# Attention with inducing points and a gated feed-forward network: the first quad over another queue, the last quad in quarters, the exponential sums as one more column, and a later schedule

## The chip, the cores and the metric

The kernel runs on one core of one Trainium2 chip. The metric is the device time of one execution in microseconds (us), and lower is better. Every number below comes from a timed execution or from the profile of one execution.

Engines are named as the profile names them: PE is the matmul engine (PEld its weight loads), DVE the vector engine, ACT the scalar engine, POOL and SP the two that also issue most of the DMAs. "x" of 2048 tokens (16 rows on each of 128 partitions) is called a quad.

## The reference

There are four batches of 12416 tokens with 128 features, 32 inducing points, and a feed-forward width of 1536.

```python
def mab(q, kv):                              # one attention, kv is key and value
    a = np.exp(scale * (q @ kv.T) - max)     # max along the row
    a /= a.sum(-1, keepdims=True) + 1e-09
    return a @ kv
h   = mab(I, x)                              # 32 inducing points look at all tokens
att = mab(x, h)                              # all tokens look at the 32 results
out = (sigmoid(att @ w_gate) * (att @ w_val)) @ w_out
```

So each batch has a first stage that must see all of x (`h`, 32 rows), and a second one that is cheap per token. The feed-forward network on 49664 tokens is nearly all of the work.

## The kernel before

Batch 0's first stage is a prologue, done as fast as the six quads of x arrive. Then come 97 output blocks of 512 tokens. A list of words, one word for each block, tells in which order PE gets its matmuls: `G` and `A`/`B` are gate and value products, small letters the output products, and `J` takes the next small job of a later batch (scores `s1`, sums `h`, scores of the second stage `s2`). The events `at(n, k, ...)` say in which block n and at which of its four steps k the other engines get their instructions.

The row of the first stage is `sum(exp * x) / sum(exp)`. The numerator is 16 matmuls of 32 output rows each, on four column tiles of PE (r = 0 to 3). The denominator is a set of four matmuls with a matrix of ones as weights, into the 128 columns beside it, so that DVE later adds 256 columns for each quad:

```python
def h_mm(ps, b, q, first, last, tail, ch=0, cs=P):
    for j in range(4):                                  # the sums
        nc.tensor.matmul(ps[:, cs:cs + P], ones[:, 0:P], a1n[(b, q)][:, j, :], ...)
    ...
    for j in range(4):
        for r in range(4):                              # exp * x
            nc.tensor.matmul(ps[r * M:(r + 1) * M, ch:ch + P],
                             a1_chunk(b, q, 4 * r + j), xqs[(b, q)][:, ts(4 * r + j, P)], ...)

def h_add(ps, b, first):                                # one add for each quad, on DVE
    nc.vector.tensor_tensor(out=haccs[b][:], in0=haccs[b][:], in1=ps[:, 0:2 * P], op=ALU.add)
```

The second stage's weights reach the feed-forward products by a long chain, called the rep chain below. There is one for each batch and each pair of quads, eleven in all after batch 0's first pair:

```python
def rep_events(n, b, d):
    put(n, 1, "s2", b, d)               # PE scores, ACT exp
    at(n + 1, 0, e2_dma, b, d)          # DMA transpose -> e2n
    at(n + 2, 0, s2_sum, b, d)          # POOL: row sums -> rs
    at(n + 3, 0, s2_rec, b, d)          # DVE:  1 / rs -> rc
    for i in range(2):
        at(n + 3, 0, a2_mul, b, d, i)   # POOL: e2n * rc -> a
        at(n + 3, 1, a2_dma, b, d, i)   # DMA transpose -> a2T
        at(n + 3, 3, rep_put, b, d, i)  # DMA to DRAM -> dt
        at(n + 4, 2, rep_get, b, d, i)  # 4 DMAs back -> rep
```

In one block out of four (5, 9, 13 and so on to 93) POOL also computes some of the gate-value products (`vt` and `x` below). Those blocks are called shared here.

The prologue's loads are issued by POOL, which casts fp32 to fp16 on the way (the cast queue): six quads, the sixth in two halves, then the three weight matrices of the network. SP issues two small fp32 loads, the inducing points and x's last 128 tokens (`xt`).

The softmax here doesn't subtract the row's maximum and nothing guards it: scores larger than these inputs give would overflow.

Of the kernel before, what the change touches and what calls it, by code (L numbers as in the profile page):

```python
# [16 lines left out]
P = 128  # L17
# [8 lines left out]
    "GAGBWGAabGBcGAfeGBdGAhBWgJG AilkjBGAJaBbGAcGBfeGAdWBhgG AilGBkGAjBGGAbaBcfGAeGdBG "  # L26
    "AhGBgiGAkljBGGAbaBcfGAGedBGh AGBgGiAGkBljGAGBabcGAeGBfdG AgGBhiGAlkjBWGAbafBJe "
    "AGBdcGhgAGilkjBJAGaWBbGAceBGfG AdhBGgAGikBljGAGaBbceAGfdGBhG AgiGBlGAkjJBGAGabBGcGAefBdJG "
    "AhBJgiAGlkBjJAGabBcfeG AGdhBgGAilkjBGGAabBcefGAdWBhgG AilkjBGGAbacBGAfGBedGAGhgBiG "
    "AlkGjBJAGBGbacGAefGBdGAJBJG AhgBGiAGklBjGAGBbafe AGdhBGgAGicBGlAGkBjJAGbWBaG "  # L30
    "AcGBfeGAdhGBgGAilWBkGAjJBGJabc AGBJfeAGdBGhgGAilkjBGGAbBJa AGceBGfAGdBhGgAGilkBjG "
    "AGBbafeAGdgGBhcGAikljBGGAabcBfG AeGBdgGAhiGBlGAkjBWGAabcBGef AGdhBGgAGilBGAGkjBWGAbacBefG "
    "AdGBhgGAilkjBGGAabBfeG AGBdcgGAhGiBlkjAGBWabcGAeBJf AGdgBGhAGilkBjAGGBabcfAGedBGgh "
    "AGikljBJGAbGBacGAfeGBdGAGhgBiG AlJBkGAjJBGAGbafBWe AGdhgBGAGiBclkjAGGBabcfAGedBGh "
    "AGgiBGkAGljBJAGBaWbcGAfeGBdg AGhiGBlGAkGBjGABWabAGcBJfG AedhBGAGgiBlkjAGGBabef "
    "AGdcBGgAGhiBkljGAGBbaceAGfdgBG AGhikBljGAGBabcGAefBWdAGhgGBi AGlkBjJGABbGacGAeGBfGAGdhBJ "
    "AGBJgiAGlkjBJAGabfBeG AdWBhgGAiGcBlkjAGGBabceAGfdBWg AGhikBGAGlBjGAGBbacfAGedBGhgG "
    "AiBGklGAjJBGAGabcfBGAGBGed AGhgBiGAGlkjBJGABWfeb AGadGBgGAhiGBcGAkljJBGAbaGcGBefG "
    "AdhGBgGAilkjBGGAabcBeGAfJBG AdGhBGAgJBiGAlGkBjGAGBabcf AGedBGgAGhilBkjGAGBbafe "
    "AGdcBGhAGgiBGkAGljBWAGBbacfG AedGgBhGAikGBljAGGBbacAGfBedG AGhgiBGAGBkljAGGBbacGAfGBedG "  # L40
    "AhgGBiGAkljBWGAabeBfG AdGBchGAgJBiGAlkjBWGAabBcfeG AGdgBhGAilkjBGGAabcBefGAdGBghG "
    "AilkjBJGAbGBacGAfGBeGAGdBhgG AiGBlkGAJjBJAGBWbaf AGedGBhGAgiGBcGAklBjWAGabBcfG "
    "AeGBdhGAgiGBlkAGjJBGAGabcBGe AGfBdGhAGgilBkjAGGBabcGAeGfBdG AhJBgGAilkjBGGAbaBfedG "
    "AcGhBgGAilkjBGGAabcBefGAdGgBhG AikljBGGAbacBGAfWBedGAhGgBiG AlkGBGAjJBGAGbaBcWGAfedBJ "
    "AGBJhgGAilkjBGAJaBbG AeWBfdGAcgGBhGAilkjBGGAabcBfeG AdgGBhGAilkjBGGAbacBGfAGedBGh "
    "AGgiBGkAGlBjJAGBGabcAGGBfG AeGdBgGAhGBikGAljBJG AefdGBaGAbhGBgGAicBGkJljAGBGbacG "
    "AfeBGdGAhgGBiGAklBjGAJbBaG AcGBfeGAdGBhgGAilkjBGGAaBJb AGcfBGeAGdhBGgAGilkBjG "
    "AGBbafeAGdhGBgGAciBkljGAGBabceG AfdGBhgGAilkjBGGAabcBeGAfGdBG AhGgBiGAlkjBGGAbaBcfGAGeBGd "
    "AGhBgGiAGlkjBGAGBefba AGdhBGgGAicBkljGAGBabcfAGedGBgG AhikBljGAGBbacGAefBWdAGhgBGi "
    "AGlkBjGAGBbacGAefGBdGAhGgBiG AlkjBGGAfeBabGAJdBhG AgGiBcGAlkjBGGAabcBfGAeWBdhG "  # L50
    "AgGBikGAljGBGAabcBefGAGBdhgG AilGkBjGAGBbacAGefdBGAGgGBhG AilBkjAGGeBfbaGAdhWBgG "
    "AicBGkGAlBJjGAGBabcGAfeBdgG AGhBikljGAGBabcGAfBWeGAdBhGgG AilkBjAGGaBbcGAefGBdGAGhBgiG "
    "AklBjGGAbaBfeGAJBdhG AgGiBcGAlkjBGGAbaBcfeGAdWhBgG AilkjBGGAabBcGAGfeBdGAhGBgiG "
    "AlkjBGGAbaBGcAGfedBGAGhGBgG AilkBjGAGefBbaGAdhBWgG AicBkljGAGBabcGAefGBdAGhgBGi "
    "AGlkjBGAGBbacGAfeBWdGAhgBGi AGlkBjGAGBbacGAefGBdGAhgGBiG AlkjBGGAfeaBbdGAgWBhiG "
    "AclkjBGGAabBcGAGfBedGAhGgBiG AlkjBGGAbaBcGAfWBedGAhGgBiG AlkjBGGAbaBcGAGBfedGAGhgiBG "
    "AkljBGGAabBfedGAgWBhcG AikljBGGAbacBGAGfeBdGAhGgBiG AlkjBGGAbaBcGAfWBedAGhgGBi "
    "AlkBGjABbAacBefdAghBilkj"
# [5 lines left out]
def kernel(  # L64
# [83 lines left out]
    xt32 = const.tile([P, C], F32, tag="xt32")  # L148
    nc.sync.dma_start(xt32[:], x[0, ds(NT0, P)])
# [6 lines left out]
    load_x(0, 0)  # L156
# [10 lines left out]
    for half in range(2):  # L167
        nc.gpsimd.dma_start(
            xl[:, ts(half, QT // 2)],
            x[0, ds((NQ - 1) * QT, QT)].rearrange("(p j) c -> p (j c)", j=QT // P)[  # L170
                :, ts(half, QT // 2)],
        )
    nc.gpsimd.dma_start(wg16[:], moe_w_gate.rearrange("c (j f) -> c j f", f=P))
# [10 lines left out]
    haccs = [pers.tile([P, 2 * P], F32, tag=f"hacc{b}", name=f"hacc_{b}") for b in range(B)]  # L184
# [63 lines left out]
    def h_mm(ps, b, q, first, last, tail, ch=0, cs=P):  # L248
        for j in range(4):
            nc.tensor.matmul(  # L250
                ps[:, cs:cs + P], ones[:, 0:P], a1n[(b, q)][:, j, :],
                start=first and j == 0, stop=last and j == 3,
            )
            if tail and j == 0:
                nc.tensor.matmul(
                    ps[:, cs:cs + M], ones[:, 0:P], a1n[(b, "t")][:], start=False, stop=False
                )
        for j in range(4):
            for r in range(4):
                nc.tensor.matmul(  # L260
                    ps[r * M:(r + 1) * M, ch:ch + P],
                    a1_chunk(b, q, 4 * r + j),
                    xqs[(b, q)][:, ts(4 * r + j, P)],
                    start=first and j == 0,
                    stop=last and j == 3 and not (tail and r == 0),
                )
        if tail:
            nc.tensor.matmul(
                ps[0:M, ch:ch + P], a1n[(b, "t")][:], xtail[:, b, :], start=False, stop=last,
            )  # L270

    def h_add(ps, b, first):
        if first:
            nc.vector.tensor_copy(out=haccs[b][:], in_=ps[:, 0:2 * P])
        else:
            nc.vector.tensor_tensor(
                out=haccs[b][:], in0=haccs[b][:], in1=ps[:, 0:2 * P], op=ALU.add
            )
# [3 lines left out]

    recs = {}

    def hfin_rec(b, sums):
        hs = smp.tile([P, M], F32, tag="hs", name=f"hs_{b}")
        nc.vector.reduce_sum(
            out=hs[:], in_=sums.rearrange("p (r m) -> p m r", m=M), axis=AX.X
        )
        rec = smp.tile([P, M], F32, tag="rec", name=f"rec_{b}")  # L290
        nc.vector.reciprocal(out=rec[:], in_=hs[:])
        recs[b] = rec

    def hfin_dve(ps, b):
        nc.vector.tensor_tensor(out=hTs[b][:], in0=recs[b][:], in1=ps[:, 0:M], op=ALU.mult)
# [284 lines left out]
    def xT_pe(b, q, half):  # L580
        ps = slot_g(f"xt_{b}_{q}_{half}")
        v = ps[:].bitcast(F16)
        for j in range(8):
            nc.tensor.transpose(
                v[:, ts(j, P)], xqs[(b, q)][:, ts(8 * half + j, P)], ident[:]
            )
        dst = xTs[b][:, ds(q * QT + half * 8 * P, 8 * P)]
        if half:
            nc.vector.tensor_copy(out=dst, in_=v[:, 0:8 * P])
        else:  # L590
# [323 lines left out]
```

## Time and profile before

| | us |
|---|---|
| median of three runs | 706.63 (705.22 to 707.18) |
| first gate product of block 0 | 28.33 |
| end of block 0 | 39.3 |
| block 12 (usual blocks: 5 to 9) | 15.06 |
| row sum h job on PE, from its first start to the next job (median of the 18 in the body) | 0.66 |
| add of 256 columns on DVE | 0.414 |

The end of a block is the end of ACT's copy of its output (`oT`). First the table by stages (the windows view) of the kernel before. Its columns are the window and its length, then busy time and number of instructions of each engine, the granted PE clock as a share of full speed, the DMA engines' share and GB/s:

```profile
core 0: us, PE busy (x) PEld busy (x) DVE busy (x) ACT busy (x) POOL busy (x), PEclk, DMA share, GB/s
8.00:12.00 4.00, 2.56 (x49) 2.22 (x49) 1.38 (x3) 2.67 (x4) 2.57 (x7) 1.00 1.07 213
...
80.00:100.00 20.00, 19.11 (x153) 6.52 (x152) 18.82 (x23) 17.64 (x22) 9.12 (x11) 1.00 0.90 147
110.00:120.00 10.00, 6.63 (x38) 1.87 (x34) 6.34 (x9) 7.89 (x9) 4.09 (x8) 0.95 1.04 158
120.00:130.00 10.00, 9.65 (x81) 3.31 (x81) 8.23 (x11) 5.98 (x7) 8.25 (x9) 0.71 0.73 161
140.00:640.00 500.00, 494.29 (x3068) 165.54 (x3067) 495.97 (x584) 492.80 (x572) 229.23 (x287) 1.00 0.61 121
```

From 140 to 640 us DVE, PE and ACT are all busy over 98% of the time: the body is full on three engines at once. From 110 to 130 us they are not full, and the clock falls. The waits of the kernel before (total, times, longest, in us), in the prologue and around that place:

```profile
PE xt_4_0_406 L584 <- DMA xq_4_132<-in_x_dram: 1.0, 1, 1.0
...
POOL tree_0_2_1811 L358 <- DMA e2n_2_1710<-e_0_2_1682: 3.8, 1, 3.8
DVE rc_2_1911 L366 <- POOL rs_2_1810 L358: 3.7, 1, 3.7
PE h_1938 L250 <- DMA a1n_2_1712<-e_1_2_1647: 3.4, 1, 3.4
```

There are two separate waits in block 12. DVE stands at the reciprocal for the row sums, which POOL makes from the transposed e2n; and PE stands at an h job for the transposed exponentials a1n_2. Both transposes are DMAs, issued at 110.1 and 111.4 us. They took 5.9 and 8.8 us to land, with the DMA share at 1.04 from 110 to 120 us. In the prologue PE waits 1.0 us for the fifth quad (xq_4).

### The profile page before, as it was taken

Reading aid. Unit: us, or ns where it says so; the run is one execution under the profiler, and the core shown is the slowest. Engines: PE = TensorE matmul, PEld = TensorE weight load, DVE = VectorE, ACT = ScalarE, POOL = GpSimd, SP = SyncE. Lnnn points to the kernel's source line nnn. Section 1 sums busy time; section 2 is a strip of 40 time slices with the busy share of each in tenths; the row PEclk is TensorE's granted clock in tenths of the full one; section 3 lists DMA queues with packets and bytes.
Section 4 is the critical chain, followed back from the end, with each engine's and each line's share of the span. In section 5 each row is a group of like instructions: output and inputs, shape, how many; then the busy total and the mean of one; then the engine's idle time right before and its main releaser. Section 6 shows DMA issues by size and latency. Waiting matters only on the chain.

```text
span 705.6 us, 13076 instructions
## 1 busy us (share of the span) xinstructions
PE 680.8 (96%) x4561; PEld 238.4 (34%) x4561; DVE 666.7 (94%) x792; ACT 662.1 (94%) x773; POOL 311.3 (44%) x404
## 2 busy tenths in 40 slices
PE   7899997999999999999999999999999999999996
PEld 4433332333333333333333333333333333333334
DVE  2599997999999999999999999999999999999997
ACT  4699987899999999999999999999999999999994
POOL 5337153535625616518615625336344345354050
PEclk9999998999999999999999999999999999999999
DMA  9678989949797794485896694352452252362232
GB/s 176 96 127 137 194 140 187 171 86 139 161 168 135 158 142 105 98 150 106 162 185 118 123 209 90 68 136 53 98 139 54 66 146 59 84 163 40 67 75 61
DMA packets 163955, 85.95 MB, mean 122 GB/s; under 512 B 133392, under 2 KB 148144, under 8 KB 163888
## 3 DMA queue, kind: packets, MB, share of 16 engines
q1 hardware_dynamic: 143904, 45.95, 36.4%
q0 software_dynamic: 19696, 39.03, 26.2%
q8 instruction: 35, 0.57, 0.3%
q14 instruction: 32, 0.26, 0.2%
q10 hardware_dynamic: 288, 0.13, 0.1%
HBM read 39.34 MB, written 28.31 MB: 96 GB/s over the span
## 4 chain that ended last, share of the span: by engine, by line
PE 72%; DVE 10%; ACT 8%; DMA 4%; issue 4%; POOL 2%; DVEq 0%; ACTq 0%; SPq 0%; POOLq 0%
DMA xq_4_132<-in_x_dram 2%; DMA a1n_2_1712<-e_1_2_1647 1%; DMA on_1324<-oT_1322 1%; PE acc_1990 L543 1%; PE acc_2481 L543 0%; PE acc_7384 L543 0%; PE acc_6824 L543 0%; PE acc_4813 L543 0%; PE acc_7646 L543 0%; PE acc_8180 L543 0%; PE acc_1040 L543 0%; PE acc_940 L543 0%; PE acc_6038 L543 0%; PE acc_4383 L543 0%; PE acc_6961 L543 0%
## 5 line engine op out<-in xcount | busy, mean ns | idle before, releaser
L543 PEld LDWEIGHTS <-wo_117 128*128 128x128 f16 x1152 | 94.1, 97 | 144.2 <-issue 90.4
L433 PEld LDWEIGHTS <-hw_168 32*128 32x128 f16 x460 | 20.6, 91 | 56.2 <-issue 53.1
L433 PEld LDWEIGHTS <-hw_167 32*128 32x128 f16 x470 | 19.5, 91 | 54.5 <-issue 52.0
L433 PEld LDWEIGHTS <-hw_165 32*128 32x128 f16 x458 | 18.6, 91 | 56.7 <-issue 54.8
L433 PEld LDWEIGHTS <-hw_166 32*128 32x128 f16 x460 | 18.8, 91 | 52.1 <-issue 50.0
L433 PEld LDWEIGHTS <-hwp_170 128*128 128x128 f16 x116 | 11.3, 98 | 17.7 <-issue 10.1
L433 PEld LDWEIGHTS <-hwp_169 128*128 128x128 f16 x118 | 11.3, 98 | 16.3 <-issue 8.3
L433 PEld LDWEIGHTS <-hwp_172 128*128 128x128 f16 x116 | 11.2, 98 | 13.3 <-issue 4.5
L433 PEld LDWEIGHTS <-hwp_171 128*128 128x128 f16 x106 | 10.3, 97 | 14.5 <-issue 8.4
L250 PEld LDWEIGHTS <-ones 128*128 128x128 f16 x96 | 7.0, 98 | 8.1 <-DMA a1n_2_1712<-e_1_2_1647 3.9
L195 PE MATMUL warm<-ones 128*128 128x512 f16 x16 | 6.0, 561 | 1.5 <-DVE ones L145 1.5
L513 POOL TENSOR_TENSOR vt_0_9918<-v_93_2_9915,T_0_9910 128x512 f32<-128x512 f32 x1 | 1.1, 1150 | 12.5 <-PE va_2_9942 L433 12.5
L315 POOL COPY hwp_169<-hw_165 32x128 f16<-32x128 f16 x2 | 0.6, 282 | 13.4 <-ACT hw_165 L308 13.3
L556 ACT ACTIVATE o_10404<-acc_10319 128x256 f32<-128x256 f32 x2 | 0.8, 383 | 5.9 <-PE acc_10319 L533 5.1
L244 ACT ACTIVATE a1nt_205<-s1t_203 128x32 f16<-128x32 f32 x1 | 0.2, 197 | 6.4 <-PE s1t_203 L240 6.4
L513 POOL TENSOR_TENSOR vt_0_8082<-v_73_2_8079,T_0_8069 128x512 f32<-128x512 f32 x1 | 1.2, 1152 | 10.6 <-ACT v_73_2_8079 L839 10.6
L513 POOL TENSOR_TENSOR vt_0_9576<-v_89_2_9573,T_0_9563 128x512 f32<-128x512 f32 x1 | 1.1, 1148 | 10.6 <-ACT v_89_2_9573 L839 10.6
L513 POOL TENSOR_TENSOR vt_0_2433<-v_17_2_2430,T_0_2420 128x512 f32<-128x512 f32 x1 | 1.2, 1152 | 9.3 <-ACT v_17_2_2430 L839 9.3
L138 POOL COPY fence_2_1334<-xT_154 128x2 f16<-128x2 f16 x1 | 0.2, 184 | 11.3 <-DMA xT_154<-xq_2_1147 11.3
L571 POOL DMA_DIRECT2D out_dram<-on_2123 x1 | 0.5, 532 | 10.4 <-DMA on_2123<-oT_2121 10.4
L513 POOL TENSOR_TENSOR vt_0_7730<-v_69_2_7727,T_0_7706 128x512 f32<-128x512 f32 x1 | 1.1, 1145 | 8.4 <-ACT v_69_2_7727 L839 8.4
L487 ACT ACTIVATE T_0_1972<-g_0_1969 128x1024 f16<-128x1024 f32 x1 | 1.0, 1023 | 4.1 <-PE g_0_1969 L433 4.1
(4296 smaller groups left out, 2803.0 us busy)
## 6 DMA issues: line engine op xcount, KB each, us to landing
xq_0_120<-in_x_dram POOLq DMA_DIRECT2D x1, 512.0 KB, 5.1
xq_1_122<-in_x_dram POOLq DMA_DIRECT2D x1, 512.0 KB, 6.9
xq_2_128<-in_x_dram POOLq DMA_DIRECT2D x1, 512.0 KB, 8.3
xq_3_130<-in_x_dram POOLq DMA_DIRECT2D x1, 512.0 KB, 10.3
xq_4_132<-in_x_dram POOLq DMA_DIRECT2D x1, 512.0 KB, 13.9
xq_5_134<-in_x_dram POOLq DMA_DIRECT2D x2, 256.0 KB, 14.4
xq_0_708<-in_x_dram POOLq DMA_DIRECT2D x1, 512.0 KB, 6.2
xq_1_933<-in_x_dram POOLq DMA_DIRECT2D x1, 512.0 KB, 7.5
```

The lines of the kernel that those rows point to most:

```text
L138: nc.gpsimd.tensor_copy(out=t[:], in_=xTs[b][:, ds(q * QT, 2)])
L195: nc.tensor.matmul(ps[:, 0:TOK], ones[:, 0:P], ones[:], start=True, stop=True)
L244: nc.scalar.activation(out=an[:], in_=ps[:, 0:M], func=AF.Exp, scale=SCALE)
L250: nc.tensor.matmul(ps[:, cs:cs + P], ones[:, 0:P], a1n[(b, q)][:, j, :], start=first and j == 0, stop=last and j == 3,)
L315: nc.gpsimd.tensor_copy(out=pads[b][rows, 2 * i + jj, :], in_=hws[b][rows, p, :])
L433: nc.tensor.matmul(ps[:, ds(col, TOK)], weights(k["b"]), rep[rows, 4 * k["i"] + k["r"]], start=True, stop=True,)
L487: nc.scalar.activation(out=Ts[(bi, p)][:, :, 0:T], in_=ps[:].rearrange("p (a t) -> p a t", a=2)[:, :, 0:T], func=AF.Tanh, scale=0.5,)
L513: nc.gpsimd.tensor_tensor(out=t[:], in0=v, in1=Ts[(bi, j0 // 2)][:, j0 % 2 + jj, :], op=ALU.mult)
L543: nc.tensor.matmul(accs[bi][:, 0:T], wo16[:, j, :], u, start=(c == 0), stop=(c == NJ - 1))
L556: nc.scalar.activation(out=o32[:, h:h + w, :].rearrange("p b c -> p (b c)"), in_=accs[bi][:, ds(h * P, w * P)], func=AF.Copy, scale=0.5,)
L571: nc.gpsimd.dma_start(out[ds(row0, QT)].rearrange("(p j) c -> p j c", j=QT // P)[:, 4 * k["r"]:4 * k["r"] + 4, :], on[:],)
```

## The change

It wants to start earlier and to wait less. The first quad goes as plain fp32 over SP's queue and is cast by DVE and ACT. The last quad comes in quarters, so that PE can begin with the first. POOL holds the weights' loads until the fourth quad has landed. The exponential sums become a 129th column of the h matmuls, so that the add has 129 columns instead of 256, and the separate ones matmuls and DVE's reduce go. The word list is new, three jobs of batch 1 have later places, and the rep chain starts half a block later at its reciprocal.

```diff
 # prologue: loads
+    for half in range(2):
+        nc.sync.dma_start(x32[:, ts(half, QT // 2)], x[0, ds(0, QT)]...)     # fp32, 2 x 512 KB
     nc.sync.dma_start(xt32[:], x[0, ds(NT0, P)])
-    load_x(0, 0)
     load_x(0, 1)
...
-    for half in range(2):                   # last quad
+    for part in range(4):
...
+    fence = const.tile([P, 2], F16, tag="fence0")
+    nc.gpsimd.tensor_copy(out=fence[:], in_=xqs[(0, NQ - 3)][:, 0:2])        # holds the weights
...
+    nc.vector.tensor_copy(out=xqs[(0, 0)][:, 0:QT // 2], in_=x32[:, 0:QT // 2])
+    nc.scalar.copy(out=xqs[(0, 0)][:, QT // 2:QT], in_=x32[:, QT // 2:QT])
     nc.vector.tensor_copy(out=xtail[:, 0, :], in_=xt32[:])
 # sums as a column
+        def pair(r, w, x, go, stop):
+            rows = ps[r * M:(r + 1) * M]
+            nc.tensor.matmul(rows[:, 0:P], w, x, start=go, stop=stop, ...)
+            nc.tensor.matmul(rows[:, P:P + 1], w, ones[:, 0:1], start=False, stop=stop, ...)
...
-    in1=ps[:, 0:2 * P]
+    in1=ps[:, 0:P + 1]
 # rep chain
-        at(n + 3, 0, s2_rec, b, d)
+        at(n + 3, 2, s2_rec, b, d)
         for i in range(2):
-            at(n + 3, 0, a2_mul, b, d, i)
-            at(n + 3, 1, a2_dma, b, d, i)
-            at(n + 3, 3, rep_put, b, d, i)
-            at(n + 4, 2, rep_get, b, d, i)
+            at(n + 3, 2, a2_mul, b, d, i)
+            at(n + 3, 3, a2_dma, b, d, i)
+            at(n + 4, 1, rep_put, b, d, i)
+            at(n + 4, 3, rep_get, b, d, i)
 # batch 1's jobs
-                s1s, s1t, fin = ((5, 0), (9, 0), (12, 3)), 6, 15
-                hs = ((8, 1), (8, 3), (12, 1), (12, 2), (14, 2), (15, 0))
+                s1s, s1t, fin = ((5, 0), (9, 2), (12, 3)), 6, 15
+                hs = ((8, 1), (8, 3), (13, 0), (13, 2), (14, 2), (15, 0))
...                                          # and a new PLAN, not shown
```

The order of PE's instructions in an h job becomes: a matmul of 128 columns, its matmul of one column, and so on for j = 0 to 3 and r = 0 to 3.

## The prediction

> **What bounds the kernel now.** Two parts. A prologue (batch 0's first attention stage) until 28.8 us, then 97 output blocks, about 677 us. In the window sums from 140 to 640 us the vector engine DVE is busy 98.6 to 99.7%, ACT 98 to 99%, PE 97.8 to 99.6%: DVE binds the body, with PE (72% of the chain) close behind. From 110 to 130 us DVE is busy only 14.6 of 20 us: it waits 3.7 us for a row sum from POOL, PE waits 3.4 us for the DMA transpose a1n_2, and the granted clock falls to 0.71 from 120 to 130 us. About 5 us are lost there. A prologue quad (2048 tokens) takes 2.15 us; PE waits 1.0 us for the fifth quad (landing 18.0 us) with the DMA share at 1.0 from 4 to 22 us.
>
> **What the change does.**
> 1. Schedule: the reciprocal moves half a block later and the h jobs that read a1n_2 most of a block later (about 7 us), while the transposes are issued at the same places. a1n_2 landed at about 120.2 us, PE wanted it at 116.8: the stall should go. Worth -4 to -5.5 us.
> 2. Sums as one column: on DVE, each h add shrinks from 256 to 129 columns (0.414 us now; about 0.29 us by slope) and the 0.29 us reduce goes: about -3 us of DVE work over 18 h jobs.
> 3. On PE the same edit costs. An h job now takes 0.65 us: four row-sum matmuls 55 ns apart, then 16 column-tiled ones, four starting within 12 ns, groups 56 ns apart. After, each is followed by a one-column matmul on the same column tile, which must wait for it, and PE starts in order; so the four tiles no longer overlap. The Trainium skill (TensorEngine Tiling (Array Packing), "Instruction Overhead") says one column costs as much as 60; the trace's 32-column matmuls start 25 ns apart. Estimate: 16 pairs x 59 ns = 0.95 us plus the mode switch, +0.4 to +0.5 us per job, 8 us of PE over 18 body jobs. The new word list adds about 11 stretches of 32-row matmuls: 2 us more. PE has about 3% slack, so I expect less than half to reach the time: +2 to +5 us.
> 4. Prologue: the first quad gives nothing by itself (PE's first transpose at 8.2 us is bound by warm-up matmuls and the inducing chain). Held weights remove the 1.0 us wait for the fifth quad. But from the third quad on each loop carries a longer h (cadence about 2.5 us instead of 2.15), and the final division gets two more fp32 matmul passes (+0.2 us). Sum: +0.5 us, between -1 and +2.5.
>
> **Sum:** -5 -3 +3.5 +0.5 = about -4 us: 702.5 us, range 696 to 708. If the pairs overlap after all, about 696.
>
> **What would show it.** Step 1: 110 to 130 us dense on DVE, no PE wait for a1n_2 above 1 us, clock 1.00 there. Step 2: adds near 0.29 us. Step 3: h jobs spanning 0.9 to 1.1 us, starts about 59 ns apart, not 14. Step 4: no wait for xq_4; hT ready at 26 to 27.5 us (now 25.7).
>
> **What would make it wrong.** One-column matmuls overlapping (better) or costing 80 ns a pair (worse); the stall reappearing at another DMA; the new word list starving DVE.
>
> Chances: faster by over 2% 0.02, within 2% 0.96, slower by over 2% 0.02.

## The result, and the profile after

The changed kernel took 726.35 us (median of four runs, 724.84 to 727.1), against 706.9 (705.22 to 708.31) for the kernel before on the same chip. The ratio is 1.0273 with a 95% interval from 1.0244 to 1.0303: slower. A ratio here is the mean time of one kernel's fast runs over the mean of the other's of the same rounds, so it isn't quite the ratio of the medians that are quoted beside it.

The same stages of the changed kernel:

```profile
core 0: us, PE busy (x) PEld busy (x) DVE busy (x) ACT busy (x) POOL busy (x), PEclk, DMA share, GB/s
8.00:12.00 4.00, 0.00 (x0) 0.00 (x0) 0.00 (x0) 1.04 (x1) 0.00 (x0) 0.93 1.10 237
...
80.00:100.00 20.00, 12.17 (x62) 3.38 (x59) 11.05 (x13) 11.29 (x14) 3.21 (x8) 0.83 0.92 170
110.00:120.00 10.00, 9.69 (x97) 3.40 (x96) 10.00 (x14) 9.32 (x11) 6.11 (x8) 1.00 0.44 76
120.00:130.00 10.00, 10.00 (x60) 3.36 (x58) 10.00 (x12) 9.96 (x12) 3.90 (x8) 1.00 0.98 168
140.00:640.00 500.00, 485.91 (x3268) 160.97 (x3266) 485.81 (x573) 484.23 (x563) 228.43 (x287) 0.99 0.64 120
```

The old stall is gone: 110 to 130 us is now full. But there are three losses. From 8 to 12 us PE does nothing at all. From 80 to 100 us all three busy engines stand for 8 to 9 us of 20. And in the long stretch DVE is busy 10 us less than before. The waits of the changed kernel name them:

```profile
PE indT L599 <- DVE xtail L595: 6.1, 1, 6.1
PE g_0_804 L431 <- DMA rep_0_729<-a2q_q_0_734: 0.9, 1, 0.9
PE xt_4_8_448 L582 <- issue: 0.8, 1, 0.8
PE h_215 L261 <- issue: 0.5, 1, 0.5
...
DVE u_2_1490 L498 <- PE vb_0_1488 L431: 8.6, 1, 8.6
ACT T_0_1486 L485 <- PE g_0_1483 L431: 8.2, 1, 8.2
PE g_0_1483 L431 <- DMA rep_1_1341<-dt_1_0_1284: 7.6, 1, 7.6
...
PE g_0_6631 L431 <- DMA rep_1_6479<-dt_1_0_6426: 2.9, 2, 2.6
```

At the start PE waits 6.1 us for a transpose of x's last tokens, because their small load `xt` stands behind 1 MB of the first quad in SP's queue and lands at 12.6 us instead of 3.0. Block 0 ends at 47.5 us instead of 39.3, so in this profile the prologue is 8.3 us late. Later PE waits for `rep`, the end of the rep chain: block 6 takes 16.48 us instead of 7.17, and block 55 takes 13.38 instead of 8.89. The summary of the chain that ended last says the same, kernel before first:

```profile
PE 72%; DVE 10%; ACT 8%; DMA 4%; issue 4%; POOL 2%; DVEq 0%; ACTq 0%; SPq 0%; POOLq 0%
```

and the changed kernel, where DMA went from 4% to 12%:

```profile
PE 66%; DMA 12%; ACT 8%; DVE 6%; issue 4%; POOL 2%; SPq 1%; DVEq 0%; ACTq 0%; POOLq 0%
```

Two parts of the change did what they were meant to. The add shrank as planned (the instructions of a tile; kernel before, then changed):

```profile
L276 DVE TENSOR_TENSOR hacc_159<-hacc_159,h_3531 x1: 414/414/414, 228.3 to 228.3; 128x256 f32<-128x256 f32 x1
```

```profile
L279 DVE TENSOR_TENSOR hacc_165<-hacc_165,h_3716 x1: 282/282/282, 243.1 to 243.1; 128x129 f32<-128x129 f32 x1
```

And an h job became shorter on PE, not longer. In the timeline (start, length, what, how many), the kernel before has the job and the start of the next:

```profile
260.19 0.39 PE L250 MATMUL h_4012<-a1n_2_3805,ones 128*128 128x128 f16 x4
260.51 0.41 PE L260 MATMUL h_4012<-xq_2_2789,a1n_2_3805 128*32 128x128 f16 x16
260.85 0.39 PE L433 MATMUL g_0_4034<-rep_1_3748,hw_166 32*128 32x512 f16 x2
```

and the changed kernel:

```profile
275.74 0.25 PE L261 MATMUL h_4220<-xq_2_2938,a1n_2_3986 128*32 128x128 f16 x4
275.81 0.19 PE L262 MATMUL h_4220<-ones,a1n_2_3986 128*32 128x1 f16 x4
275.84 0.24 PE L261 MATMUL h_4220<-xq_2_2938,a1n_2_3986 128*32 128x128 f16 x4
...
276.21 0.39 PE L431 MATMUL va_2_4254<-rep_1_3951,hw_172 32*128 32x512 f16 x2
```

From the first start to the next job it takes 0.47 us here instead of 0.66. Over the 18 h jobs of the body the median is 0.48 us instead of 0.66, and the shortest 0.43 instead of 0.65. The reason is in the order of the starts. The program has long, short, long, short (the program as built has PE's instructions in this order too, so no compiler moved them); the trace starts four long ones within 20 ns, then the four short ones, and only then the next four. So PE's starts pass one another across column tiles. From the first of the four long ones to the first short one it takes 55 ns as a rule, and from there to the next long one 26: about 81 ns for four pairs, where the prediction had 59 ns for each pair. The Trainium skill's page "TensorE: Matmul & The Clock Gate" (Part 3, "The mechanism") says that matmuls are monotone in program order in start and end. This trace disagrees about the starts: the second instruction of the program, a short one, starts 46 ns after the seventh. The ends, which the profile models, are still in program order. The prediction had leaned on the starts ("PE starts in order").

### The profile page after: what moved, and what is told of

Same layout as the page of the kernel before. It is cut to its first block, busy times and chain, and to the rows that moved or that the text cites. A ratio compares the mean times of both kernels' runs of the same rounds, so it can differ in the third digit from the quotient of the medians.

```text
span 725.2 us, 13685 instructions
## 1 busy us (share of the span) xinstructions
PE 680.7 (94%) x4857; PEld 237.1 (33%) x4857; DVE 666.0 (92%) x792; ACT 663.2 (91%) x775; POOL 312.0 (43%) x406
## 4 chain that ended last, share of the span: by engine, by line
PE 66%; DMA 12%; ACT 8%; DVE 6%; issue 4%; POOL 2%; SPq 1%; DVEq 0%; ACTq 0%; POOLq 0%
DMA xt_113<-in_x_dram 1%; DMA rep_1_6479<-dt_1_0_6426 1%; DMA a2T_1_1_1259<-a_0_1_1_1226 1%; DMA xq_5_1868<-in_x_dram 1%; DMA rep_1_3951<-dt_1_0_3898 1%; DMA dt_2_0_2137<-a2T_2_0_2104 1%; DMA rep_2_4845<-dt_2_0_4770 1%; DMA xT_160<-xq_5_1868 1%; DMA xq_4_1657<-in_x_dram 1%; DMA a2T_2_0_2104<-a_0_2_0_2076 1%; DMA xT_160<-xq_4_1657 1%; DMA rep_0_729<-a2q_q_0_734 1%; DMA rep_1_1341<-dt_1_0_1284 0%; PE acc_8978 L541 0%; PE acc_2633 L541 0%
## 5 line engine op out<-in xcount | busy, mean ns | idle before, releaser
L511 POOL TENSOR_TENSOR vt_0_10223<-v_93_2_10220,T_0_10210 128x512 f32<-128x512 f32 x1 | 1.2, 1152 | 12.4 <-PE va_2_10242 L431 12.4
L511 POOL TENSOR_TENSOR vt_0_4699<-v_37_2_4696,T_0_4648 128x512 f32<-128x512 f32 x1 | 1.1, 1147 | 9.2 <-ACT v_37_2_4696 L839 9.2
L511 POOL TENSOR_TENSOR vt_0_9503<-v_85_2_9500,T_0_9484 128x512 f32<-128x512 f32 x1 | 1.1, 1144 | 9.1 <-ACT v_85_2_9500 L839 9.1
## 6 DMA issues: line engine op xcount, KB each, us to landing
xq_4_134<-in_x_dram POOLq DMA_DIRECT2D x1, 512.0 KB, 13.6
```

Of the source, the lines that this page charges most:

```text
L511: nc.gpsimd.tensor_tensor(out=t[:], in0=v, in1=Ts[(bi, j0 // 2)][:, j0 % 2 + jj, :], op=ALU.mult)
```

## The experiments

Three theories stood at the start. A: SP's queue order at the start (`xt` behind 1 MB) makes the prologue's loss. B: the rep chain's later places make the loss in the body, since the multiply `a` on POOL now stands behind the shared products. C, the rival that the prediction would have named: the column sums cost PE time (the expectation of experiment 4 uses "theory C" for the opposite, that they save it). Sixteen kernels ran, in five calls, each call on another chip. Each call timed the kernel before as well, with medians of 705.87, 706.23, 706.36, 707.32 and 706.38.

### 1. Only the small load first

```diff
+    nc.sync.dma_start(xt32[:], x[0, ds(NT0, P)])     # moved up, before the first quad
     for half in range(2):
         nc.sync.dma_start(x32[...], x[0, ds(0, QT)]...)
-    nc.sync.dma_start(xt32[:], x[0, ds(NT0, P)])
```

> The changed kernel with one line moved: the 64 KB load of batch 0's tail tokens (xt32) is issued before the two 512 KB fp32 halves of the first quad on the sync queue, as in the kernel before. Theory A (the tail load stood in line behind 1 MB on its own queue: landed 12.6 us, PE idle 6.1 us, then half clock from 12 to 18 us): xt32 lands by 3.5 us, PE no longer waits for it, and the next bound is ACT's cast of the second half (begins 9.85 us), so the first transposes start near 7 to 8 us, the first output matmul moves from 35.7 to 31 to 33 us, total 722 to 724 us. Rival (the fp32 landing of the quad, or the held weights, cost the time): first output matmul stays within 1 us of 35.7.

Measured: 727.63 us (725.87 to 729.85), ratio 1.0308 (1.028 to 1.0336). A in this form fell, and the rival held: the first gate product stayed at 35.7 us. `xt` landed at about 3 us, but the halves of the first quad landed at 9.7 and 13.6 us instead of 5.7 and 9.8, PE still waited 3.9 us for `xtail` (now behind DVE's cast of the first half) and 2.5 us for ACT's cast of the other, and block 0 ended at 47.6 us. The megabyte in fp32 is late by itself. The queues of SP and POOL share the same DMA engines, which are full: the Trainium skill says so ("DMA: Bandwidth & Descriptors", "Issuing engines are not separate DMA queues"), and here the second half came at 13.6 us with the DMA share at 1.04 to 1.09 from 8 to 14 us, where the kernel before had the whole first quad at 6.4 us on the cast queue alone.

### 2. The first quad back on the cast queue

```diff
-    (the two fp32 halves and their casts)
+    load_x(0, 0)
```

> The changed kernel with the first quad loaded as before (one casting DMA on the POOL queue, no cast on chip); held weights and the last quad in quarters stay. Theory A (the whole prologue loss comes from the first quad's new path): first output matmul at 27 to 28.5 us (28.3 in the kernel before), total 718 to 720 us. Rival (held weights or the quarters cost too): first output matmul later than 29 us. Theory of my prediction (longer h cadence): quads at 2.5 us instead of 2.15 us.

Measured: 723.74 us (720.83 to 728.17), ratio 1.0254 (1.0202 to 1.0306). The first 21 us are then as in the kernel before, so the queue was a loss, of about 2.6 us in medians. The four runs spread over 7.3 us, so this pair alone does not settle the size; experiments 3 and 5 differ in the same edit, by 2.4 us, and their ratios' intervals do not overlap. But the rival was right as well: the first gate product came at 34.3 us and block 0 still ended at 45.2, 5.9 late. The profile shows why. PE stood for 2.4 us in the middle of an h job, with no semaphore to wait for ("issue"), and then the clock fell. The waits and the stages of this kernel:

```profile
PE h L254 <- issue: 2.4, 1, 2.4
```

```profile
20.00:22.00 2.00, 1.95 (x90) 1.71 (x90) 0.85 (x2) 0.88 (x2) 0.47 (x1) 1.00 1.09 214
22.00:24.00 2.00, 0.00 (x0) 0.00 (x0) 0.00 (x0) 0.00 (x0) 0.00 (x0) 0.98 1.45 183
24.00:26.00 2.00, 1.60 (x20) 1.23 (x21) 0.64 (x2) 0.28 (x1) 0.00 (x0) 0.50 0.94 98
```

After the gap PE ran at half clock from 24 to 34 us. A new question: what stops PE where no semaphore does?

### 3. The rep chain back at its old places

```diff
-        at(n + 3, 2, s2_rec, b, d)   ... a2_mul (n+3, 2), a2_dma (n+3, 3), rep_put (n+4, 1), rep_get (n+4, 3)
+        at(n + 3, 0, s2_rec, b, d)   ... a2_mul (n+3, 0), a2_dma (n+3, 1), rep_put (n+3, 3), rep_get (n+4, 2)
```

> The changed kernel with only the softmax normalisation events (reciprocal, multiply, transpose, put, get) back at their old places, half a block earlier; word list, h and s1 places of the changed kernel stay. Theory B (the multiply now queues on POOL behind three shared products and everything after it is late, so PE waits for rep: gaps 8.0, 1.7, 3.0, 0.6 us): no PE gap above 0.5 us at a first use of rep, total 711 to 716 us. Rival (the old events bring the old stall back, 3.7 us on DVE for the row sum and 3.4 us on PE for a1n): a stall of over 2 us near 120 to 130 us, total 718 to 722 us.

Measured: 709.02 us (707.97 to 710.11), ratio 1.0043 (1.0023 to 1.0063). Theory B holds, with a larger gain than it expected (711 to 716): about 17 us of the loss are the rep chain (17.3 between the medians, 16.2 by the ratios), and no wait for `rep` is left. Block by block, the two profiles part at block 6 (9.4 us), block 14 (2.3 us), and twice more by block 60. POOL's and DVE's timelines show the way. In the kernel before, the multiply follows the reciprocal at once (DVE's line first, then POOL's):

```profile
59.67 0.35 DVE L366 RECIPROCAL rc_1_1077<-rs_1_976 128x32 f32<-128x32 f32 x1
60.43 1.06 POOL L375 TENSOR_TENSOR a_0_1_0_1079<-e2n_1_881,rc_1_1077 128x512 f16<-128x512 f16 x1
```

In the changed kernel three shared products (a `vt` and an `x` each, 2.4 to 2.6 us together) stand between:

```profile
71.82 1.26 POOL L514 TENSOR_TENSOR x_0_1185<-vt_0_1186,v_5_2_1183 128x512 f16<-128x512 f32 x1
...
76.97 1.27 POOL L514 TENSOR_TENSOR x_2_1213<-vt_2_1214,v_5_1_1211 128x512 f16<-128x512 f32 x1
78.20 1.04 POOL L373 TENSOR_TENSOR a_0_1_0_1224<-e2n_1_968,rc_1_1222 128x512 f16<-128x512 f16 x1
...
71.91 0.35 DVE L364 RECIPROCAL rc_1_1222<-rs_1_1066 128x32 f32<-128x32 f32 x1
```

The gap from reciprocal to multiply grew from 0.4 to 5.9 us; it is 4 to 6.2 us in eight of the eleven chains. Behind it the two transposes landed at 81.7 and 89.2, the writes to DRAM at 89.6 and 90.9 and the first piece of `rep` at 96.3 us. The second transpose alone took 8.7 us (2.4 in the kernel before), beside the next load of batch 1, which POOL issued at 80.3, just after the multiply. PE had wanted the piece 7.6 us earlier. In the kernel before, that first piece landed at 76.6 us and was used at 80.5.

### 4. The kernel before with the column sums alone

```diff
 # before.py, with h_mm, h_add and hfin of the changed kernel, in prologue and body; nothing else
```

> The kernel before with only the sums as one more column (h jobs, adds of 129 columns, the final division from two matmuls); loads, schedule and word list of before. The prediction's step 3 (pairs serialise, h job +0.4 us, +2 to +5 us in total, less 3 us of DVE): 705 to 709 us. Theory C, from the trace of the changed kernel (four long matmuls overlap, then four short ones, 81 ns per group of four pairs, h job about 0.2 us shorter than before): 702 to 705 us.

Measured: 710.82 us (709.37 to 711.9), ratio 1.0067 (1.0044 to 1.009). Slower than either side had expected. In the body its h jobs take 0.50 us in the median, so the cost that the prediction's step 3 forecast isn't there; one wait of 2.5 us for a transposed quad fell into block 8. The prologue lost 3.6 us (block 0 at 42.9), again with a gap without a semaphore. PE's timeline:

```profile
22.54 0.22 PE L251 MATMUL h<-xq,a1q 128*32 128x128 f16 x1
22.59 0.16 PE L252 MATMUL h<-ones,a1q 128*32 128x1 f16 x1
24.16 0.25 PE L251 MATMUL h<-xq,a1q 128*32 128x128 f16 x4 [1.40 <-issue]
```

I counted PE's instructions (loads of weights and matmuls, and two records ahead of them) in the order of their starts up to each such gap, and looked at the packets of 16384 bytes on the queue that the page names "q8 instruction":

```text
kernel                     last start, next   after instruction   last instruction packet ended
changed                    24.19 to 25.16     449                 23.70
                           27.91 to 28.62     705                 27.34
2 (quad on cast queue)     21.79 to 24.40     705                 23.03
3 (rep chain old)          23.99 to 24.90     449                 23.54
                           27.66 to 28.64     705                 27.18
4 (column sums only)       22.59 to 24.16     705                 22.80
before                     none               705 reached 26.4    23.34
```

Every gap is at 449 or 705, which are 256 apart, and ends 1.3 to 1.5 us after an instruction packet has ended. (Experiment 1 has its gaps at the same two, experiment 7 at 705.) The Trainium skill ("Runtime: NRT & Kernel Launch", "Instruction fetch mechanics") says that an engine's instructions are fetched in 16 KiB blocks of 256 by a DMA queue of its own, and that this is mostly hidden. Here it isn't hidden. The column sums make an h job 64 PE instructions instead of 40, so PE comes to number 705 about 4 us earlier than in the kernel before (22.6 against 26.4 us).

Full DMA engines are not needed for it. In the changed kernel they are all but idle around the gap at 705 (27.91 to 28.62 us):

```profile
26.00:28.00 2.00, 2.00 (x100) 1.82 (x91) 1.21 (x3) 0.84 (x2) 0.00 (x0) 1.00 0.03 8
```

The times of the packets say when the next block is asked for. In the kernels where PE passed 449 with nearly idle DMA engines (changed, 1 and 3: a share of 0.23 and less from 25.2 us on) the packet began 1.1 to 1.2 us later, and instruction 706 started 3.5 to 3.7 us after 450. Where x was still arriving (2, 4, 5, 7 and 8) the packet began 3.2 to 3.6 us after 450, and 706 started 5.5 to 5.9 us after it. So 256 instructions look as if they were asked for when PE starts the 256 before them, and PE stands when it gets through those faster than the next ones come. This is read from the times; no run tested it alone.

### 5. Both losses undone

```diff
 # changed kernel, with the edits of experiments 2 and 3 together
```

> The changed kernel with the first quad loaded by the cast queue again and the rep events at their old places; quarters, held weights and column sums in the prologue stay. Theory: both losses add, so the time is that of the third experiment (709.0) less what the second saved (about 2.6): 705 to 708 us, and the prologue still ends block 0 near 45 us, with PE standing at its 705th instruction without a semaphore. Rival: the prologue's remainder belongs to the late rep events: block 0 at 40 us and about 700 us.

Measured: 706.65 us (705.99 to 706.89), ratio 1.0001 (0.9984 to 1.0017). The two add up as expected. Block 0 ended at 44.2 us, and PE stood from 22.53 to 24.17 us after its 705th instruction, until 1.25 us after a packet's end.

### 6. Everything of the prologue old, body as changed

```diff
 # changed kernel, with rep chain, loads, prologue and row sums of batch 0 as before
```

> The changed body (word list, later h and s1 places, sums as a column) with the prologue and the rep events of the kernel before. Theory: the changed prologue (+8 us) and the late rep chain (+17 us) are the whole loss, and the rest of the change is a gain of 6 to 8 us, nearly all of it the old stall at 110 to 130 us. Then block 0 ends at 39.3 to 40.3 us, block 12 takes about 9 us and the time is 697 to 702 us. Rival: the gain in the body of the third experiment came from its late start (loads and rows already there, POOL less behind), and an early start gives it back: 704 us or more.

Measured: 704.51 us (702.24 to 705.56), ratio 0.9969 (0.9947 to 0.9991). The profile agrees with the theory (block 0 at 40.3, block 12 at 8.47 us), but the median misses the expected 697 to 702: the gain is 0.3%. The profiled execution was the quickest of the four. What varies came out only in experiments 12 to 16. The median lies in the rival's range, 704 us or more, and a late start does spare experiment 5 this scatter: its four runs lie within 0.9 us.

### 7. The multiply early, the transfers late

```diff
-            at(n + 3, 1, a2_dma, ...)   rep_put (n+3, 3)   rep_get (n+4, 2)      # of experiment 5
+            at(n + 3, 3, a2_dma, ...)   rep_put (n+4, 1)   rep_get (n+4, 3)
```

> As the previous kernel, but of the rep chain only the reciprocal and the multiply on POOL go back to their old place; the transposes, the write to DRAM and the read back stay two to three steps late as in the change. Theory: the loss comes from the multiply standing in POOL's order behind three products of 6 us; then the gap from reciprocal to multiply is again about 0.4 us, no rep wait is over 2.6 us, and the time is within 3 us of the previous kernel. Rival: the late transfers make the loss: rep waits of 5 us and more remain at block 6, and the time is at least 9 us above the previous kernel.

Measured: 711.3 us (709.88 to 715.13), ratio 1.0078 (1.0048 to 1.0108), so 4.7 us above experiment 5. Neither side is right alone. The gap from the reciprocal's end to the multiply is under 0.5 us in nine of eleven chains (1.0 and 2.0 in the others), and PE's largest wait for `rep` is 1.7 us instead of 7.6. So the place of the reciprocal and the multiply is the larger part of the 17 us (about 12), and the later transfers are the rest (about 5). In the profile, which is of the slowest of the four runs, that rest is not the wait for `rep` alone: DVE also waits 3.0 us for row sums near block 12, which it does not in experiment 5 (1.2 us at most).

### 8. More PE instructions in the old prologue

```diff
 # before.py, prologue only: behind each of the 16 h matmuls of a quad
+                nc.tensor.matmul(ps[r * M:(r + 1) * M, ch + P:ch + P + 1], a1_chunk(b, q, 4 * r + j),
+                                 ones[:, 0:1], start=False, stop=False, ...)   # a column nobody reads
```

> The kernel before, with one matmul of one column of ones more behind each of the 16 h matmuls of a prologue quad, into an unread column: 32 PE instructions more per quad, nothing else changed, right results. Theory: PE runs out of instructions when it reaches an instruction that is a multiple of 256 (plus 193) before its block of 16 KB has landed, because the DMA engines are full with x; then PE stands 1 us or more, without a semaphore, at instruction 449 or 705 until 1.2 to 1.6 us after such a packet ends, the clock falls to 0.5 some 2 to 5 us later, block 0 ends 2 to 5 us later than 39.3 us, and the time is 708 to 711 us. Rival: the stall in the kernels with column sums has to do with the column sums (their mode, their accumulator); then no such gap, block 0 within 1 us, and 706 to 707.5 us.

Measured: 710.67 us (709.93 to 712.14), ratio 1.0063 (1.0048 to 1.0078), results right, block 0 at 41.4 us. The gap appeared where the fetch theory put it, between two of four equal matmuls that wait for nothing:

```profile
23.46 0.27 PE L274 MATMUL h<-a1q,ones 128*128 128x128 f16 x2
24.20 0.27 PE L274 MATMUL h<-a1q,ones 128*128 128x128 f16 x2 [0.47 <-issue]
```

It is after instruction 705, and it ends 1.41 us after a packet's end at 22.79. So the gap isn't the column sums' mode or their accumulator: it comes with the number of PE instructions before a given time. The gap is not the whole loss here, though. In this profile PE also waited 1.6 us for the fifth quad, the clock was at 0.50 for 3.4 us after that, and experiments 6, 9 and 15, which have such a wait without the additional matmuls, end block 0 at 40.1 to 40.3 us. One part of the expectation missed: the gap was 0.7 us and the clock did not fall after it. Over these profiles the half clock came some microseconds after each gap of 1.6 us and more (experiments 2, 4, 5 and 7), and did not come after the gaps of 0.7 and 1.0 us in the changed kernel; but in experiment 3 it came after one of 1.0 us, from 32 to 38 us. Waits for the fifth quad show the same: after those of 1.5 to 1.8 us (experiments 5, 6, 7, 8, 9, 12 and 15) the clock was at 0.50 for 3.4 us, after those of 1.0 to 1.2 us (before, 2, 4, 10 and 16) it stayed at 1.00. So the length of the gap says most, and in experiment 3 it does not settle it.

### 9. Column sums in the body alone

```diff
 # before.py, column sums for batches 1 to 3; batch 0 keeps its row sums
```

> The kernel before with the sums as a column in the body's 18 h jobs alone; batch 0's prologue keeps its row sums, so PE's first 1000 instructions are those of before. Theory: the loss of the kernel with column sums throughout (710.8) came from the prologue and one unlucky wait, and in the body the column is a gain on both engines (h job 0.43 us against 0.65 on PE, add 0.29 against 0.41 us plus no reduce on DVE); then block 0 ends at 39 to 40.3 us and the time is 702.5 to 705.5 us. Rival: the shorter jobs reach the time nowhere, since other waits end last: 705.5 to 708 us.

Measured: 704.1 us (703.58 to 706.26), ratio 0.9977 (0.9961 to 0.9993). A small gain. In the profile, which started 0.8 us late, the body gained 4.3 us to the end of block 95 (from +0.8 to -3.5).

### 10. The last quad held

```diff
 # before.py
+    fence = const.tile([P, 2], F16, tag="fence0")
+    nc.gpsimd.tensor_copy(out=fence[:], in_=xqs[(0, NQ - 3)][:, 0:2])
     xl = xqp.tile(...)                     # the sixth quad's halves, then the weights
```

> The kernel before with one more edit: POOL waits for the fourth quad before it issues the sixth quad's halves (and so the weights). In before the fifth quad landed at 17.96 us, 4.1 us after the fourth, and the first half of the sixth at 18.56: their packets of 4096 and 2048 bytes alternate from 15 us on. Theory: the wait for the fifth quad comes from the sixth quad sharing the engines, not from the weights, which is why holding the weights did nothing; then the fifth quad lands at 16.2 to 17.0 us, PE's wait for it is under 0.4 us, and the time falls by 0.5 to 1.5 us at most (PE may stand at instruction 705 instead). Rival: the fifth quad is slow by itself: landing 17.5 us or later, wait 0.9 us or more, time as before.

Measured: 706.22 us (705.36 to 708.09), ratio 1.0004 (0.9988 to 1.0019). The fifth quad landed at 17.34 us, between what the two sides expected, and the time did not move. The packets of the queues give another answer. A quad counts as landed when all 16 DMA engines have written their part and added to the semaphore, as the Trainium skill has it ("DMA: Bandwidth & Descriptors", "Why a DMA increments its semaphore by 16 and not by 1"); the trace has these writes as packets of 4 bytes:

```text
kernel            16 KB packet of PE's instructions   writes of the fifth quad          landed
before            15.91 to 16.84                      15 by 15.94, the last after 16.5  17.96
6                 15.84 to 16.78                      15 by 15.94, the last after 16.7  17.89
11                16.08 to 17.04                      16 by 15.90                       16.24
14                16.42 to 17.35                      16 by 16.07                       16.36
```

In these four, when the instruction packet begins before the quad is complete, the last write is late and the quad lands at 17.9 or 18.0; when it begins after, the quad is there 1.6 us earlier. The same holds where the writes can be told apart in the other profiles: in seven more (4, 8, 9, 10, 12, 15 and 16) 15 writes come together and the quad is late, and in experiment 13 all 16 do and it is early. So PE's own instruction fetch is the likely maker of the wait for the fifth quad. The link is by time in these traces; no run moved the packet alone, and experiment 13 has a packet that began early and delayed nothing. The weights have no part in it, and holding them could not help: with the fence of the changed kernel the fifth quad landed at 18.03 us in experiment 5.

### 11. The later places alone

```diff
 # before.py
-                s1s, s1t, fin = ((5, 0), (9, 0), (12, 3)), 6, 15
-                hs = ((8, 1), (8, 3), (12, 1), (12, 2), (14, 2), (15, 0))
+                s1s, s1t, fin = ((5, 0), (9, 2), (12, 3)), 6, 15
+                hs = ((8, 1), (8, 3), (13, 0), (13, 2), (14, 2), (15, 0))
```

> The kernel before with only the later places of batch 1's second score job and of the third and fourth h jobs; word list, sums, loads, rep events as before. Theory: the places alone remove the stall at 110 to 130 us (PE no longer wants a1n_2 before it has landed), and the new word list adds nothing: block 12 takes 8.5 to 10 us instead of 15.1, time 700.5 to 703 us. Rival: the word list is needed too, the job only waits at another letter: block 12 takes over 12 us and the time is 704 us or more.

Measured: 710.16 us (708.58 to 713.28), ratio 1.0066 (1.0047 to 1.0085). The rival is right. With the old word list the new places only swap two jobs, and the score job that now comes first waits for another DMA:

```profile
PE s L773 <- DMA xT<-xq: 6.7, 1, 6.7
```

Block 12 took 17.79 us. The places need the new list.

### 12. Experiment 6 with the last quad held

```diff
 # experiment 6, with the edit of experiment 10
```

> The best version so far (changed body, prologue and rep events of before: 704.5 us) with the sixth quad held as in the second kernel of this call. In that version's profile PE stood 1.9 us for the fifth quad and the clock was 0.57 from 20 to 22 us. Theory: with no such gap the clock stays 1.00 until 28 us, block 0 ends at 38.5 to 39.5 us and the time is 702 to 704 us, below both kernels. Rival: PE then runs into the instruction fetch at 449 or 705 and stands there as long: block 0 at 40 us or later and 704 to 706 us.

Measured: 701.35 us (699.81 to 707.5), ratio 0.9942 (0.9913 to 0.9972). The median is in the range of the theory, but not for its reason. The fifth quad landed at 17.92 us as ever, and block 0 ended at 40.3. The profiled execution was the slowest of the six, at 707.5, and it took 23.2 us for blocks 11 and 12 where experiment 6's profile took 17.5. Its waits there:

```profile
POOL tree L390 <- DMA e2n<-e: 6.9, 1, 6.9
...
DVE rc L398 <- POOL rs L390: 5.2, 1, 5.2
```

This is the other half of the old stall, DVE's wait for the row sums. The changed kernel's later reciprocal is what takes it away. With the reciprocal back at its old place it comes in some executions, longer or shorter.

### 13 and 14. One late rep chain out of eleven, with and without the hold

```diff
 # experiment 6 (14), and with the edit of experiment 10 (13)
+        o = 2 if (b, d) == (0, 2) else 0
-        at(n + 3, 0, s2_rec, b, d)
+        at(n + 3, o, s2_rec, b, d)
 ...             # a2_mul, a2_dma, rep_put, rep_get later by o steps too (the change moved rep_get by one)
```

> The best version without the held quad (changed body, prologue of before, rep events of before: 702.2 to 705.6 us in four runs), with the late places of the change for one rep event of eleven, that of batch 0's last pair of quads. In slow executions of its sister kernel DVE waited 5.2 us at 110 to 125 us for the row sum rs on POOL, whose tree waited 6.9 us for the transposed e2n. Theory: the late reciprocal is what takes that wait off DVE, and this one event has the slack for it; then blocks 11 and 12 together take at most 17.5 us in every profile, no wait of DVE for rs is over 1 us there, and the time is 700.5 to 702.5 us with a spread under 3 us. Rival: the late chain is a loss for this event too (rep wait at blocks 16 and 17), 704 us or more.

> As the previous kernel, with the sixth quad's halves held for the fourth quad besides. Theory: the hold does nothing for the prologue (the fifth quad's 1.7 us come from PE's own 16 KB instruction packet on one of the 16 DMA engines, not from the sixth quad), so the fifth quad lands 1.0 to 1.2 us after the end of that packet in both kernels, and the times of both agree within 0.2%. Rival: the hold is worth the 3 us by which its sister kernel was faster than the version without it (701.35 against 704.51): 698 to 700 us here, and 1.5 us or more below the previous kernel.

Measured: 704.68 us (702.13 to 705.76), ratio 0.9962 (0.994 to 0.9983) without the hold, and 704.38 us (702.03 to 706.9), ratio 0.9967 (0.9944 to 0.999) with it. So the hold is worth nothing, and the time of neither fell to the 700.5 to 702.5 that the theory of 14 expected. The profile with the hold also shows that a packet may begin early and yet delay nothing: it ran from 15.51 to 16.41, and the quad landed at 16.32. Blocks 11 and 12 took 16.5 and 16.1 us, as the theory had it. But block 14 took 12.05 and 10.41 us instead of 7.9, with a new wait in the kernel without the hold:

```profile
PE g L463 <- DMA rep<-dt: 2.4, 1, 2.4
```

Two steps of a block are too many for this chain.

### 15 and 16. One step instead of two, and experiment 6 again

```diff
-        o = 2 if (b, d) == (0, 2) else 0
+        o = 1 if (b, d) == (0, 2) else 0
```

> As the version with one late rep event, but that event moves by one step of a block instead of two, so that the multiply does not stand behind all of POOL's shared products. Two steps took the wait for rs away (blocks 11 and 12 together 16.1 and 16.5 us) but made a rep wait of 2.0 to 2.4 us at block 14 (10.4 and 12.1 us instead of 7.9). Theory: one step is enough for rs and leaves the rep in time; blocks 11 and 12 at most 18 us together, block 14 under 8.6 us, median 699.5 to 702 us. Rival: what one wait gives the other takes as long as the DMA engines are full here: 703 us or more.

> The best version without hold or late event once more, beside the previous kernel: its four runs spread over 3.4 us and its sister with the hold, which does not touch this place, over 7.7. Theory: the spread is the wait for rs at 110 to 125 us, which is there in some executions; median 702 to 705 us with a spread of 3 us or more, above the previous kernel by 1 us or more. Rival: no difference between the two, within 0.1%.

Measured: 700.23 us (699.89 to 701.38, five runs), ratio 0.9916 (0.9897 to 0.9935), for the one step; 703.45 us (700.3 to 705.75), ratio 0.9957 (0.9929 to 0.9984), for experiment 6 again. The one step keeps both: blocks 11 and 12 took 16.3 us together (20.9 in experiment 6 again) and block 14 took 7.93. No wait of DVE for rs is left there, nor any for `rep` in the body, and the spread of the five times is 1.5 us against 5.5. The fifth quad scatters too: the one program of experiments 6 and 16 waited 1.7 and 1.2 us for it and ended block 0 at 40.3 and 38.6 us, and the one-step kernel's profile still has the long wait (1.8 us, block 0 at 40.2). The stages of the one-step kernel at the old stall:

```profile
110.00:120.00 10.00, 9.86 (x55) 3.23 (x53) 10.00 (x12) 10.00 (x12) 3.21 (x6) 1.00 1.21 150
120.00:130.00 10.00, 9.29 (x117) 3.02 (x116) 8.91 (x13) 8.44 (x11) 9.64 (x10) 1.00 0.82 166
```

This is the fastest version of the sixteen, below both kernels: 0.8% below the kernel before and 3.6% below the changed one (26.1 us of 726.35, between medians of different calls).

## Why the prediction was wrong, point by point

It said 702.5 us, 696 to 708, and 2% for slower by over 2%. The time was 726.35.

The losses and gains, from medians of different calls:

| part of the change | us | from |
|---|---|---|
| rep chain later, all eleven | +17.3 | changed against experiment 3 |
| first quad in fp32 on SP's queue | +2.4 to +2.6 | 3 against 5, changed against 2 |
| column sums, quarters and held weights in the prologue | +2.1 to +3.2 | 5 against 6 and 16 |
| body: word list, places, column sums | -1.7 to -2.9 | 6 and 16 against the kernel before |

The last two rows hold for kernels 6 and 16, which wait for row sums at block 12 in some executions, while the later start of 5 spares it that wait. Against experiment 15, which has no such wait, the third row is +6.4 us and the fourth, with the one chain moved, -6.2. And the column sums in the prologue, on the schedule of the kernel before, cost 6.7 us (4 against 9; 2.5 of them are the one wait in block 8).

- **Step 1, schedule, -4 to -5.5 us.** Right in its first half: the stall at 110 to 130 us went, block 12 fell from 15.06 to 8.98 us, the clock stayed at 1.00, and no wait for a1n_2 is left (one of 1.8 us for the next, a1n_4, came at 152 us). It failed in what it left out. It booked the later reciprocal as a gain alone, and put no cost on the four lines of the diff that move the multiply, the transposes, the write and the reads with it. The multiply fell behind 6 us of shared products on POOL, and at block 6 the chain's end came 7.6 us after PE wanted it: +17.3 us in all, the largest single error and the step that failed. "The stall reappearing at another DMA" stood among the things that would make it wrong, and that is what happened.
- **Step 2, smaller adds, -3 us.** The size was right: 0.283 us for the add instead of 0.414, where 0.29 was estimated. With step 3's part the column sums in the body are worth 2.3 us in medians (experiment 9; the interval of the ratio allows 0.5 to 2.7).
- **Step 3, one-column matmuls serialize on PE, +2 to +5 us.** Wrong, and in sign. PE's starts are not in program order across column tiles; an h job takes 0.48 us in the median instead of 0.66, and not 0.95. The prediction's own "if the pairs overlap after all" was the case.
- **Step 4, prologue, +0.5 us.** Wrong in size: block 0 was 8.3 us late in the profile, and `hT` was ready at 33.1 us instead of 26 to 27.5. It held that the first quad gives nothing, and missed that it takes: its megabyte in fp32 lands late on full DMA engines and holds up `xt`. It held that held weights remove the wait for the fifth quad, which stayed at 1.0 to 1.5 us in experiments 2 and 5 (in the changed kernel PE came too late to wait for it). Its longer cadence of 2.5 us did not come: with the column sums alone (experiment 4) the first two h jobs start 2.1 us apart, as before. It counted the column sums' time on PE and not their number: 24 more PE instructions for each quad make PE run into its own instruction fetch, and each gap of 1.6 us or more was followed by some microseconds at half clock.

What stays open: the parts that quarters and held weights have in the third row were not run alone. The rule that joins the instruction packet to the fifth quad's landing, and the reading that a block of instructions is asked for when PE starts the one before, rest on the times in the profiles.

## What to carry to other kernels

When a diff moves a chain of events later, write down for each instruction of the chain what it will now stand behind on its engine, and when its last product is needed; a half block on paper became 17 us here, while one step at the one place that needed it is a gain. Where PE stops with "issue" and no semaphore, count its instructions: here the gaps stood 256 instructions apart, at instruction fetch, and more small instructions in a short time cost more than they computed. Before a wait is put down to what shares a queue, look at which of a load's last packets came late.

## What the Trainium skill lacked or had wrong

- "TensorE: Matmul & The Clock Gate" (Part 3, "The mechanism") has matmuls monotone in program order in start. With pairs of 128 columns and 1 column on four column tiles the trace starts four long, then four short ones, though the program alternates them; 16 pairs take 0.43 us at the least. The modelled ends stay in program order.
- "TensorEngine Tiling (Array Packing)" ("Instruction Overhead") says that a matmul with one column costs as much as with 60. The trace fits this for four tiles together: from the first of four one-column matmuls to the next long one it takes about 26 ns, where 128 columns take 55, so 60 would take about 26 by proportion (an estimate). What the section lacks is that four column tiles share that cost, so that the 16 one-column matmuls of a job cost it about four times 26 ns and not 16 times.
- "Runtime: NRT & Kernel Launch" ("Instruction fetch mechanics") calls the fetch mostly hidden. Here it cost PE 0.7 to 2.6 us at a time, at instructions 449 and 705, ending 1.2 to 1.5 us after a 16 KB packet's end, and in the changed kernel also with the DMA share at 0.03. The page gives no time for a block: here 256 instructions took 3.5 to 3.7 us to come with nearly idle DMA engines and 5.5 to 5.9 with full ones, and PE's small matmuls, at 7 to 25 ns from start to start, were quicker.
- "DMA: Bandwidth & Descriptors" does not mention that an engine's instruction packet (0.9 us on one of the full DMA engines) may hold up the last of the 16 parts of a load: the fifth quad landed at 17.9 and 18.0 us with it ahead, and at 16.2 and 16.4 us with it behind.
- "TensorE: Matmul & The Clock Gate" (Part 1) puts the cold clock after an idle window of about 3.4 us. Here shorter gaps on PE were enough: a clock of 0.50 followed for 6 us and more after the gaps at instruction 705 of 1.6 us and more in experiments 2, 4 and 5, and for 3.4 us after waits of 1.5 to 1.8 us for the fifth quad in seven profiles (and in experiment 3 after a gap of 1.0 us, while gaps of 0.7 to 1.2 us in other kernels were not followed by it).
